# Text gate rows moved into the text output's run of 32-column matmuls, with P of batch 0 transposed ahead of text V

## The chip, the core and the metric

The kernel runs on one core of a Trainium2 chip. The metric is the device time of one execution in microseconds (us). A core has a matmul engine (TensorE, PE in the profile, with its weight loads shown as PEld), a vector engine (DVE), a scalar engine (ACT), GpSimd (POOL) and SyncE (SP); here SP does nothing but issue DMAs. Each engine works through its own queue in order and waits for the others by semaphores. Matmul results go to PSUM, and DVE and ACT bring them from there to SBUF.

## The reference

One attention block over two streams of tokens, image and text, for a batch of 2, with 256 image tokens, 32 text tokens and D = 1152, all in bf16. Each stream has its own weights and its own modulation (shift, scale and gate) from a condition vector `c`.

```
mod_i = (silu(c) @ wmod_img)            # shift, scale, gate of the image
mod_t = (silu(c) @ wmod_txt)            # shift, scale, gate of the text
hi = layernorm(x_img) * (1 + sci) + shi
ht = layernorm(x_txt) * (1 + sct) + sht
q, k, v = concat of (ht @ wqkv_txt, hi @ wqkv_img)
p = softmax(q @ k^T * D**-0.5)
a = p @ v                               # at: text rows, ai: image rows
out_i = x_img + gai * (ai @ wo_img)
out_t = x_txt + gat * (at @ wo_txt)
```

## The kernel before

The reduction dimension D is cut into KT = 9 blocks of 128. All weights come in blocks of 1152 x 1152 (2592 KB) through five SBUF slots, asked for by SP in the order of lines 80 to 122; a load waits in SP's queue until the last reader of its slot is done, and the loads behind it wait too. The last ones are the image gate (slot 0, free when DVE has read the text shift weights), text V (slot 1), the text gate (slot 2, free after text Q), the image output weights `w_o_i` (slot 3, three row groups, free after text K) and the text output weights `w_o_t` (slot 1 again, free after text V).

The order of PE's work is written out by hand: every matmul and transpose goes through `mm` (line 61) or `tr` (line 64), which pin it to program order. After image scale and V (to about 35 us) come image Q and K (`qk_img`, lines 372 to 380), with hooks between their nine column blocks at which the text preparation is put in: `txt_ln` (LayerNorm statistics on DVE), `txt_shift_part` (lines 413 to 419: the text shift vector made on DVE as 18 products of weight rows with a scalar, 1.4 us each), `txt_shift_split`, `txt_rows_scale`, `txt_rows_shift`, `txt_modulate`. Then text Q and K, and, from 77 us on, the part that matters here, in this order on PE: scores of batch 0, scores of the text rows of both batches, image gate rows, scores of batch 1, text V, transposes of P of batch 0 and of batch 1, text gate rows, attention, and the output of the four image tiles with the text output between the third and the fourth.

Work with few columns of weights is tiled over the array: the 128 columns are split into strips of 64 or 32, and matmuls with different strips run side by side. Gate rows (`mod_rows`, lines 496 to 506) multiply the silu columns `sT32` (32 columns, two of them used) with the gate weights, four strips of 288 output columns, 9 blocks: 36 matmuls. Their result stands in PSUM as a row per batch and strip, goes to SBUF (`g_sb`), from there to a DRAM scratch `gsc` by POOL's DMAs, and back as a broadcast over partitions: `gb` for the image, `gbf` for the text, where partition 64g + 32b + t holds the gate values of text token t of batch b for column group g. The text output (`out_txt`, lines 656 to 671) uses two strips of 64 columns (both batches' 32 tokens in one), two runs of 9 blocks, 18 matmuls each; DVE multiplies by `gbf`, adds `xf` (the text input in the same layout) and two DMAs write it out.

P is normalised by DVE per tile (`softmax_tile`: `nmx`, then ACT's `e` with its row sum, then `rs` and two products into `pb`). `p_transposes(b)` makes nine transposes of the two image tiles and the text tile into one PSUM tile, copied to `pT` by DVE for batch 0 and by ACT for batch 1. `v_txt` evicts its four parts alternately by DVE and ACT into `v_t`, and DVE copies `v_t` to a second set of partitions. In `attn_pair` (three output tiles of each batch at a time) the key matmuls of batch 0 come first, then six matmuls with `v_t`, batches 0 and 1 in turn, then the key matmuls of batch 1.

The scheduler orders what is not pinned (evictions, DMAs) by program order and dependences. PSUM has six buffers for matmul results (`ps_mm`) and two for transposes and strips (`ps_tr`).

Of the kernel before, what the change touches and what calls it, by code (L numbers as in the profile page):

```python
# [14 lines left out]
def kernel(  # L15
# [14 lines left out]
    nc = tc.nc  # L30
    bf = mybir.dt.bfloat16
    f32 = mybir.dt.float32
    PSUM = bass.MemoryType.PSUM

    B, NI, D = x_img.shape
    NT = x_txt.shape[1]
    P = 128
    KT = D // P
# [3 lines left out]
    NTT = B * NT  # L42
    CH = 384
    NCH = D // CH
    VC = 288
# [7 lines left out]
    work = ctx.enter_context(tc.tile_pool(name="work", bufs=2))  # L53
    small = ctx.enter_context(tc.tile_pool(name="small", bufs=4))
    ps_mm = ctx.enter_context(tc.tile_pool(name="ps_mm", bufs=6, space=PSUM))
    ps_tr = ctx.enter_context(tc.tile_pool(name="ps_tr", bufs=2, space=PSUM))
# [3 lines left out]
    def mm(*a, **k):  # L60
        return pin(nc.tensor.matmul(*a, **k))  # L61

    def tr(*a, **k):
        return pin(nc.tensor.transpose(*a, **k))  # L64
# [11 lines left out]
    def wtile(slot):  # L76
        return wpool.tile([P, KT, D], bf, tag="w%d" % slot, name="t")

    def wview(src, c0):
        return src.rearrange("(kt p) n -> p kt n", p=P)[:, :, c0:c0 + D]  # L80
# [3 lines left out]
    def load_w(slot, src, c0, splits=(D,)):  # L84
        t = wtile(slot)
        sv = wview(src, c0)
        o = 0
        for n in splits:
            nc.sync.dma_start(t[:, :, o:o + n], sv[:, :, o:o + n])
            o += n  # L90
        return t

    def load_rows(slot, src, c0):
        t = wtile(slot)
        sv = wview(src, c0)
        for r0 in range(0, KT, 3):
            nc.sync.dma_start(t[:, r0:r0 + 3, :], sv[:, r0:r0 + 3, :])
        return t
# [13 lines left out]
    w_q_i = load_w(3, wqkv_img, 0)  # L112
    w_sh_t = load_rows(0, wmod_txt, 0)
    w_k_i = load_w(4, wqkv_img, D)
# [2 lines left out]
    w_k_t = load_w(3, wqkv_txt, D)  # L117
    w_ga_i = load_w(0, wmod_img, 2 * D)
    w_v_t = load_w(1, wqkv_txt, 2 * D)
    w_ga_t = load_w(2, wmod_txt, 2 * D)  # L120
    w_o_i = load_rows(3, wo_img, 0)
    w_o_t = load_rows(1, wo_txt, 0)

    nc.scalar.preload_act_table_set("natural_log_exp_and_others")
# [4 lines left out]
    NGG = 4  # L129
# [12 lines left out]
    sT32 = const.tile([P, KT, 32], bf)  # L142
# [39 lines left out]
    def evac(out_ap, in_ap):  # L182
        if evac_idx[0] % 2 == 0:
            nc.vector.tensor_copy(out_ap, in_ap)  # L184
        else:
            nc.scalar.copy(out_ap, in_ap)  # L186
        evac_idx[0] += 1
# [36 lines left out]
    def group(w, kt, g):  # L224
        return w[:, kt, :].rearrange("p (c g l) -> p g c l", g=NGG, l=LW)[:, g]
# [140 lines left out]
    def qk_evac(out_ap, in_ap, blk):  # L366
        if blk == 0:
            nc.scalar.mul(out_ap, in_ap, SCALE)  # L368
        else:
            nc.scalar.copy(out_ap, in_ap)  # L370

    def qk_img(wq, blk, hooks):
        for j in range(KT):
            for hook in hooks.get(j, ()):
                hook()
            ps = ps_mm.tile([P, B * NI], f32, tag="mm")
            for kt in range(KT):
                mm(ps[:], lhsT=wq[:, kt, j * P:(j + 1) * P], rhs=hT_i[:, kt, :],
                   start=(kt == 0), stop=(kt == KT - 1))
            qk_evac(qkT[:, blk * KT + j, :, 0:NI], ps[:].rearrange("p (b n) -> p b n", b=B), blk)  # L380

    gsc = tc.dram_tile([2, B, D], bf, name="mod_scratch")
    sel = const.tile([P, NGG, NTT], bf)
    nc.gpsimd.tensor_scalar(sel[:].rearrange("p g (b t) -> p g b t", b=B),
                            ident[:].rearrange("p (g r) -> p g r", g=NGG)[:, :, 0:B].unsqueeze(3)
# [55 lines left out]
    def txt_shift_part(r0, r1):  # L441
        return lambda: vec_part(nc.vector, w_sh_t, acc_sh, r0, r1, range(B))
# [38 lines left out]
    def v_txt():  # L481
        for r in range(2):
            ps = ps_mm.tile([P, KT, LW], f32, tag="mm")
            for kt in range(KT):
                for g in range(2):
                    mm(ps[64 * g:64 * g + NTT], lhsT=hT_t[:, kt, :], rhs=group(w_v_t, kt, 2 * r + g),
                       start=(kt == 0), stop=False, tile_position=(0, 64 * g))
            for g in range(2):
                mm(ps[64 * g:64 * g + NTT], lhsT=sel[:, 2 * r + g, :], rhs=svr[:],
                   start=False, stop=True, tile_position=(0, 64 * g))  # L490
            for g in range(2):
                evac(v_t[0:NTT, :].rearrange("p (c g l) -> p g c l", g=NGG, l=LW)[:, 2 * r + g],
                     ps[64 * g:64 * g + NTT])
        nc.vector.tensor_copy(v_t[64:64 + NTT, :], v_t[0:NTT, :])

    def mod_rows(w_blk, si):
        gps = ps_mm.tile([P, VC], f32, tag="mm")
        for kt in range(KT):
            for g in range(NGG):
                mm(gps[32 * g:32 * g + 32, :], lhsT=sT32[:, kt, :], rhs=w_blk[:, kt, g * VC:(g + 1) * VC],  # L500
                   start=(kt == 0), stop=(kt == KT - 1), tile_position=(0, 32 * g))
        g_sb = work.tile([P, VC], bf, tag="garow")
        evac(g_sb[:], gps[:])
        for b in range(B):
            nc.gpsimd.dma_start(gsc[si, b, :].rearrange("(g j) -> g j", g=NGG), g_sb[b:P:32, :])  # L505

    gb = act.tile([P, B, D], bf, tag="Bt")
    gbf = act.tile([P, 2, VC], bf)
    xf = act.tile([P, 2, VC], bf)

    def img_gate():
        mod_rows(w_ga_i, 0)
        for b in range(B):
            nc.gpsimd.dma_start(gb[:, b, :], gsc[0, b, :].partition_broadcast(P))

    def txt_gate():
        mod_rows(w_ga_t, 1)
        for g in range(2):
            pin(nc.gpsimd.dma_start(xf[64 * g:64 * g + NTT, :, :],
                                    xt_flat.rearrange("t (r g j) -> g t r j", r=2, g=2)[g]))  # L520
            for b in range(B):
                r0 = 64 * g + 32 * b
                nc.gpsimd.dma_start(gbf[r0:r0 + NT, :, :],
                                    gsc[1, b, :].rearrange("(r g j) -> g r j", r=2, g=2)[g].partition_broadcast(NT))

    v_last()
    shift_v_rows()
    qk_img(w_q_i, 0, {1: (txt_ln,), 2: (txt_shift_part(0, 3),), 5: (txt_shift_part(3, 6),),
                      6: (txt_transposes,), 8: (txt_shift_part(6, KT),)})
    qk_img(w_k_i, 1, {1: (txt_shift_split,),  # L530
                      6: (txt_rows_scale, txt_rows_shift, txt_cols_shift, txt_modulate),
                      8: (lambda: qk_txt(0, w_q_t),)})
    qk_txt(1, w_k_t)
# [1 line left out]
    aT = act.tile([P, KT, B * NTOK], bf, tag="Q")  # L535
# [19 lines left out]
    def scores_img(b):  # L555
        for qi in range(TPB):
            q0 = qi * P
            sps = ps_mm.tile([P, NTOK], f32, tag="mm")
            for ft in range(KT):
                mm(sps[:], lhsT=qkT[:, ft, b, q0:q0 + P], rhs=qkT[:, KT + ft, b, :],  # L560
                   start=(ft == 0), stop=(ft == KT - 1))
            softmax_tile(sps, P, (b, qi), [(0, P, b)])
# [15 lines left out]
    def p_transposes(b):  # L578
        pT_ps = ps_tr.tile([P, 8 * P], bf, tag="tr")

        def one(kj, pb, qp, perm):
            o = kj * NTOK + qp
            tr(pT_ps[:, o:o + P], pb[:, kj * P:(kj + 1) * P], perm[:])

        for kj in range(3):
            if b:
                one(kj, pbs["t"], qpos[b][2], ident2)
            for qi in range(TPB):
                one(kj, pbs[(b, qi)], qpos[b][qi], ident)
            if not b:  # L590
                one(kj, pbs["t"], qpos[b][2], ident)
        pT_v = pT_ps[:, 0:3 * NTOK].rearrange("p (k n) -> p k n", k=3)
        pT = work.tile([P, 3, NTOK], bf, tag="pT")
        if b == 0:
            nc.vector.tensor_copy(pT[:], pT_v)
        else:
            nc.scalar.copy(pT[:], pT_v)
        pTs[b] = pT
# [29 lines left out]
    scores_img(0)  # L628
    scores_txt()
    img_gate()  # L630
    scores_img(1)
    v_txt()
    p_transposes(0)
    p_transposes(1)
    txt_gate()
    for d0 in range(0, KT, 3):
        attn_pair(*[[(b, dt) for dt in range(d0, d0 + 3)] for b in range(B)])

# [17 lines left out]

    def out_txt():
        of = work.tile([P, 2, VC], bf, tag="of", bufs=1)
        for r in range(2):
            ps = ps_mm.tile([P, VC], f32, tag="mm")  # L660
            for dt in range(KT):
                for g in range(2):
                    c0 = (2 * r + g) * VC
                    mm(ps[64 * g:64 * g + NTT, :], lhsT=aT[:, dt, NI:NI + NTT], rhs=w_o_t[:, dt, c0:c0 + VC],
                       start=(dt == 0), stop=(dt == KT - 1), tile_position=(0, 64 * g))
            tmp = work.tile([P, CH], bf, tag="tmp")
            nc.vector.tensor_mul(tmp[:, 0:VC], ps[:], gbf[:, r, :])
            nc.vector.tensor_add(of[:, r, :], tmp[:, 0:VC], xf[:, r, :])
        for g in range(2):
            eng = nc.sync if g == 0 else nc.scalar  # L670
            eng.dma_start(ot_flat.rearrange("t (r g j) -> g t r j", r=2, g=2)[g], of[64 * g:64 * g + NTT, :, :])
# [37 lines left out]
```

## Time and profile before

| what | value |
|---|---|
| median of 9 executions | 119.88 us (118.7 to 120.3) |
| the profiled execution | 120.22 us |
| its span, first to last instruction on the core | 118.1 us |
| PE busy | 110.8 us (94%) |
| DVE, ACT, POOL busy | 75.8, 41.8, 11.2 us |
| read from HBM | 39.38 MB, about 410 GB/s from 10 to 95 us |

The times in the profile's views run from the span's start; the execution's own time is 2.1 us more than the span. PE's granted clock is full throughout. Rows of the timeline give start, length, engine, line, operation, tiles and count; a bracket gives the idle time ahead of the row on that engine and what ended it. A matmul's length is longer than the distance to the next one, since matmuls are pipelined: costs are read from start to start.

### The profile page before, as it was taken

To read this page: it belongs to the slowest core of one execution; us is meant where nothing else is said; L and a number is where in the kernel's file an instruction comes from. 1 tells how busy PE (TensorE), PEld (TensorE's weight loads), DVE (VectorE), ACT (ScalarE), POOL (GpSimd) and SP (SyncE) were. 2 spreads that over 40 slices of the span, in tenths; PEclk is the share of its full clock that TensorE was granted. 3 is DMA by queue.
4 is the path that set the end of the run, shared out by engine and by line. 5 is a ranking of instruction groups with operands and counts; after the bars stand their busy time and mean duration, and the time that the engine had idled before them with its cause. 6 is when DMAs were issued, how large, how long until landed. Compare 5 with 4: busy or idle time off the path is not lost.

```text
span 118.1 us, 2512 instructions
## 1 busy us (share of the span) xinstructions
PE 110.8 (94%) x1046; PEld 63.9 (54%) x1054; DVE 75.8 (64%) x161; ACT 41.8 (35%) x87; POOL 11.2 (9%) x34
## 2 busy tenths in 40 slices
PE   4987799999999999999999999899999999999990
PEld 1334544445574445444444557776886566556660
DVE  2668394063866799999999740018696666666571
ACT  4899520031762423423319232245454620000000
POOL 7410000000000000000000000000409008000000
PEclk9999999999999999999999999999999999999999
DMA  3999999999999999999999999999999998320223
GB/s 112 375 391 401 404 405 411 412 412 412 412 399 373 412 412 410 405 411 413 411 413 349 381 410 410 406 414 404 414 397 412 411 394 341 138 94 11 100 50 100
DMA packets 18613, 40.86 MB, mean 346 GB/s; under 512 B 1019, under 2 KB 1547, under 8 KB 18603
## 3 DMA queue, kind: packets, MB, share of 16 engines
q1 hardware_dynamic: 17728, 39.56, 86.4%
q0 software_dynamic: 480, 0.89, 2.1%
q10 hardware_dynamic: 395, 0.26, 0.7%
q8 instruction: 8, 0.13, 0.4%
q14 instruction: 2, 0.02, 0.0%
HBM read 39.38 MB, written 1.34 MB: 345 GB/s over the span
## 4 chain that ended last, share of the span: by engine, by line
PE 85%; DMA 9%; DVE 1%; issue 1%; SPq 1%; DVEq 0%
PE ps L61 52%; PE vps L61 15%; DMA t<-in_wmod_img_dram 9%; PE gps L61 6%; PE aps L61 5%; PE sps L61 4%; PE pT_ps L64 1%; PE sc_ps L61 1%; SPq L104 1%; PE tp L64 1%; DVE tmp L650 1%; DVE o L651 0%; SPq L108 0%; PE tpt L64 0%; DVE hS_i L268 0%
## 5 line engine op out<-in xcount | busy, mean ns | idle before, releaser
L61 PE MATMUL ps<-xT_i,t 128*128 128x512 bf16 x157 | 35.4, 379 | 0.3
L61 PEld LDWEIGHTS <-t 128*128 128x128 bf16 x324 | 20.6, 98 | 19.6 <-issue 0.9
L419 DVE SCALAR_TENSOR_TENSOR acc_sh<-t,sTf,acc_sh 128x1152 f32<-128x1152 bf16 x16 | 21.4, 1413 | 0.0
L61 PE MATMUL ps<-t,aT 128*128 128x384 bf16 (+3 forms) x153 | 20.2, 308 | 0.0
L61 PE MATMUL vps<-t,hS_i 128*128 128x512 bf16 (+1 forms) x106 | 17.8, 325 | 0.2
L61 PEld LDWEIGHTS <-aT 128*128 128x128 bf16 (+1 forms) x153 | 13.0, 101 | 7.1 <-issue 0.5
L61 PEld LDWEIGHTS <-hS_i 128*128 128x128 bf16 x108 | 8.9, 97 | 8.8 <-DVE hS_i L268 0.4
L650 DVE TENSOR_TENSOR tmp<-ps,gb 128x384 bf16<-128x384 f32 (+2 forms) x13 | 6.8, 526 | 6.4 <-PE ps L61 6.3
L368 ACT ACTIVATE qkT<-ps 128x512 bf16<-128x512 f32 (+2 forms) x11 | 6.2, 561 | 11.8 <-PE ps L61 11.8
L370 ACT CAST qkT<-ps 128x512 bf16<-128x512 f32 (+2 forms) x11 | 5.9, 552 | 11.4 <-PE ps L61 11.4
L505 POOL DMA_DIRECT2D mod_scratch<-g_sb x4 | 2.6, 642 | 76.4 <-ACT g_sb L186 76.3
L61 PE MATMUL wps<-warm 128*128 128x512 bf16 x24 | 7.0, 446 | 1.6 <-DVE unit L132 1.5
L184 DVE CAST v_i<-vps 128x512 bf16<-128x512 f32 x5 | 3.5, 692 | 7.5 <-PE vps L61 7.5
L542 DVE TENSOR_REDUCE nmx<-sps 128x1 f32<-128x288 f32 x4 | 1.7, 449 | 9.4 <-PE sps L61 9.4
L61 PEld LDWEIGHTS <-sT 128*32 128x32 bf16 x180 | 4.7, 96 | 3.2 <-issue 2.4
L186 ACT CAST v_i<-vps 128x512 bf16<-128x512 f32 x4 | 2.3, 579 | 9.9 <-PE vps L61 9.9
L61 PE MATMUL gps<-t,sT 128*32 128x288 bf16 x144 | 5.5, 287 | 0.1
L61 PE MATMUL ps<-hT_t,t 128*128 128x64 bf16 x162 | 5.2, 193 | 0.4 <-issue 0.4
L61 PE MATMUL sps<-qkT 128*128 128x288 bf16 (+1 forms) x54 | 5.5, 287 | 0.0
L610 DVE TENSOR_SCALAR aT<-aps,svc 128x288 bf16<-128x288 f32 x9 | 4.3, 517 | 1.6 <-PE aps L61 1.6
L61 PEld LDWEIGHTS <-warm 128*128 128x128 bf16 x25 | 2.5, 110 | 5.0 <-issue 1.9
L61 PE MATMUL aps<-pT,v_i 128*128 128x288 bf16 x36 | 5.1, 287 | 0.0
(112 smaller groups left out, 107.5 us busy)
## 6 DMA issues: line engine op xcount, KB each, us to landing
t<-in_wqkv_txt_dram SPq DMA_DIRECT2D x3, 2592.0 KB, 17.8
t<-in_wmod_img_dram SPq DMA_DIRECT2D x2, 2592.0 KB, 11.8
t<-in_wqkv_img_dram SPq DMA_DIRECT2D x2, 2592.0 KB, 20.1
t<-in_wmod_txt_dram SPq DMA_DIRECT2D x2, 2592.0 KB, 16.1
t<-in_wmod_txt_dram SPq DMA_DIRECT2D x3, 864.0 KB, 15.0
t<-in_wo_img_dram SPq DMA_DIRECT2D x3, 864.0 KB, 12.8
t<-in_wo_txt_dram SPq DMA_DIRECT2D x3, 864.0 KB, 11.9
t<-in_wqkv_img_dram SPq DMA_DIRECT2D x3, 576.0 KB, 8.7
```

Source lines behind the costliest of these rows:

```text
L61: return pin(nc.tensor.matmul(*a, **k))
L64: return pin(nc.tensor.transpose(*a, **k))
L104: nc.sync.dma_start(x_i[:, b * TPB:(b + 1) * TPB, :], x_img[b].rearrange("(p t) d -> p t d", t=TPB))
L184: nc.vector.tensor_copy(out_ap, in_ap)
L186: nc.scalar.copy(out_ap, in_ap)
L368: nc.scalar.mul(out_ap, in_ap, SCALE)
L370: nc.scalar.copy(out_ap, in_ap)
L419: pin(eng.scalar_tensor_tensor(acc[:, b, :], w[:, kt, :], sTf[:, kt, b:b + 1], acc[:, b, :], op0=ALU.mult, op1=ALU.add))
L505: nc.gpsimd.dma_start(gsc[si, b, :].rearrange("(g j) -> g j", g=NGG), g_sb[b:P:32, :])
L542: nc.vector.reduce_max(nmx[0:qn, :], sps[0:qn, :], axis=AX.X, negate=True)
L610: nc.vector.tensor_scalar(dst, tiles[(b, dt)][:], bias, None, op0=ALU.add)
L650: nc.vector.tensor_mul(tmp[:, 0:n], ps[:, 0:n], gb[:, b, c0:c0 + n])
```

## The change

- The text gate rows are no longer made after the P transposes. `txt_gate` is gone; what is left of it, `txt_x`, loads `xf` by POOL ahead of the scores of batch 1. The text part of the scratch and its DMAs are gone.
- In `out_txt` the gate rows come first (36 matmuls in four strips of 32 columns), ACT copies them to `g_sb`, and the output's rows are made in four strips of 32 columns (36 matmuls in each of the two runs, for 18 strips of 64). Between the two runs, selector matmuls with `sel` (entries -1 at the row of strip and batch) spread the gate rows over the partitions, four for each run, and ACT multiplies them by -1 into `gbf`.
- P of batch 0 is transposed right after the scores of batch 1, ahead of text V.
- The load of `w_o_i` goes ahead of that of the text gate weights in SP's queue.
- At the hooks of image Q and K, the first three weight rows of the text shift come ahead of the text LayerNorm, and the text transposes go from image Q to image K.

```diff
     w_v_t = load_w(1, wqkv_txt, 2 * D)
+    w_o_i = load_rows(3, wo_img, 0)
     w_ga_t = load_w(2, wmod_txt, 2 * D)
-    w_o_i = load_rows(3, wo_img, 0)
     w_o_t = load_rows(1, wo_txt, 0)
...
-    gsc = tc.dram_tile([2, B, D], bf, name="mod_scratch")
+    gsc = tc.dram_tile([1, B, D], bf, name="mod_scratch")
...
-    def txt_gate():
-        mod_rows(w_ga_t, 1)
+    def txt_x():
         for g in range(2):
             pin(nc.gpsimd.dma_start(xf[64 * g:64 * g + NTT, :, :],
                                     xt_flat.rearrange("t (r g j) -> g t r j", r=2, g=2)[g]))
-            for b in range(B):
-                r0 = 64 * g + 32 * b
-                nc.gpsimd.dma_start(gbf[r0:r0 + NT, :, :],
-                                    gsc[1, b, :].rearrange("(r g j) -> g r j", r=2, g=2)[g].partition_broadcast(NT))
...
-    qk_img(w_q_i, 0, {1: (txt_ln,), 2: (txt_shift_part(0, 3),), 5: (txt_shift_part(3, 6),),
-                      6: (txt_transposes,), 8: (txt_shift_part(6, KT),)})
-    qk_img(w_k_i, 1, {1: (txt_shift_split,),
+    qk_img(w_q_i, 0, {1: (txt_shift_part(0, 3),), 3: (txt_ln,), 4: (txt_shift_part(3, 6),),
+                      7: (txt_shift_part(6, KT),)})
+    qk_img(w_k_i, 1, {1: (txt_transposes, txt_shift_split,),
                       6: (txt_rows_scale, txt_rows_shift, txt_cols_shift, txt_modulate),
                       8: (lambda: qk_txt(0, w_q_t),)})
...
     img_gate()
+    txt_x()
     scores_img(1)
+    p_transposes(0)
     v_txt()
-    p_transposes(0)
     p_transposes(1)
-    txt_gate()
...
     def out_txt():
         of = work.tile([P, 2, VC], bf, tag="of", bufs=1)
-        for r in range(2):
+        gps = ps_tr.tile([P, VC], f32, tag="tr")
+        for kt in range(KT):
+            for g in range(NGG):
+                mm(gps[32 * g:32 * g + 32, :], lhsT=sT32[:, kt, :], rhs=w_ga_t[:, kt, g * VC:(g + 1) * VC],
+                   start=(kt == 0), stop=(kt == KT - 1), tile_position=(0, 32 * g))
+        g_sb = work.tile([P, VC], bf, tag="garow")
+        nc.scalar.copy(g_sb[:], gps[:])
+        quads = [(g, b, 64 * g + NT * b) for g in range(2) for b in range(B)]
+
+        def rows_of(r):
             ps = ps_mm.tile([P, VC], f32, tag="mm")
             for dt in range(KT):
-                for g in range(2):
+                for g, b, r0 in quads:
                     c0 = (2 * r + g) * VC
-                    mm(ps[64 * g:64 * g + NTT, :], lhsT=aT[:, dt, NI:NI + NTT], rhs=w_o_t[:, dt, c0:c0 + VC],
-                       start=(dt == 0), stop=(dt == KT - 1), tile_position=(0, 64 * g))
+                    mm(ps[r0:r0 + NT, :], lhsT=aT[:, dt, NI + NT * b:NI + NT * (b + 1)], rhs=w_o_t[:, dt, c0:c0 + VC],
+                       start=(dt == 0), stop=(dt == KT - 1), tile_position=(0, r0))
+            return ps
+
+        def gate_of(r):
+            gp = ps_tr.tile([P, VC], f32, tag="tr")
+            for g, b, r0 in quads:
+                mm(gp[r0:r0 + NT, :], lhsT=sel[:, 2 * r + g, NT * b:NT * (b + 1)], rhs=g_sb[:],
+                   start=True, stop=True, tile_position=(0, r0))
+            nc.scalar.mul(gbf[:, r, :], gp[:], -1.0)
+
+        def finish(r, ps):
             tmp = work.tile([P, CH], bf, tag="tmp")
             nc.vector.tensor_mul(tmp[:, 0:VC], ps[:], gbf[:, r, :])
             nc.vector.tensor_add(of[:, r, :], tmp[:, 0:VC], xf[:, r, :])
+
+        ps = rows_of(0)
+        gate_of(0)
+        gate_of(1)
+        finish(0, ps)
+        finish(1, rows_of(1))
```

## The prediction

> **What bounds the kernel now.** I read the page's head and chain first, then the chain in order of time, then the timeline from 60 us on. In the first fence PE is busy for 94% of the span and the chain that ended last is 85% PE.
>
> ```profile
> span 118.1 us, 2512 instructions
> PE 110.8 (94%) x1046; PEld 63.9 (54%) x1054; DVE 75.8 (64%) x161; ACT 41.8 (35%) x87; POOL 11.2 (9%) x34
> ...
> PE 85%; DMA 9%; DVE 1%; issue 1%; SPq 1%; DVEq 0%
> ```
>
> The chain in order of time (start, length, what) shows where the change lies: text V, the P transposes, the text gate rows and attention follow one another on PE with no other engine between, and from 94.90 us PE alone runs to the tail.
>
> ```profile
> 84.12 2.57 PE ps L61 x40
> 86.69 1.11 PE pT_ps L64 x18
> 87.80 1.22 PE gps L61 x36
> 89.01 5.88 PE aps L61 x54
> 94.90 19.52 PE ps L61 x144
> ```
>
> So a matmul taken out or put in counts in full, unless it covers a wait. The timeline (start, length, engine, what; single starts named below are read from the same trace) gives the prices and, on DVE and ACT, what the gate rows cover today.
>
> ```profile
> 64.46 1.29 PE L61 MATMUL gps<-t,sT 128*32 128x288 bf16 x36
> ...
> 65.57 0.66 PE L61 MATMUL gps<-hl,pick 128*32 128x288 bf16 x16
> ...
> 83.61 0.49 DVE L551 TENSOR_SCALAR pbt<-e,rs 32x64 bf16<-32x64 f32 x2
> 84.04 1.00 PEld L61 LDWEIGHTS <-hT_t 128*64 128x64 bf16 x18 [0.24 <-issue]
> ...
> 85.31 0.16 DVE L547 RECIPROCAL rs<-rs 128x1 f32<-128x1 f32 x1 [0.35 <-ACT e L545]
> 85.51 0.35 DVE L549 TENSOR_SCALAR pb<-e,rs 128x256 bf16<-128x256 f32 x1
> ...
> 87.05 0.76 ACT L186 CAST v_t<-ps 64x288 bf16<-64x288 f32 x2 [1.28 <-DVE v_t L184]
> ...
> 87.33 0.61 DVE L595 COPY pT<-pT_ps 128x864 bf16<-128x864 bf16 x1
> ...
> 87.83 0.88 ACT L597 COPY pT<-pT_ps 128x864 bf16<-128x864 bf16 x1
> ...
> 89.79 0.42 PE L61 MATMUL aps<-pT,v_t 32*128 32x288 bf16 x6
> ...
> 107.99 2.10 PEld L61 LDWEIGHTS <-aT 128*64 128x64 bf16 x36 [0.32 <-issue]
> ```
>
> Two things are to be seen. First, four 32-column strips run side by side: 36 matmuls of 288 columns take 65.57 - 64.46 = 1.11 us, nine sets of four at 0.123 us, and a set of two 64-column strips costs as much (18 loads from 84.04 to the next form at 85.05). Second, ACT copies P of batch 1 (87.83 to 88.71) while PE makes the gate rows (87.73 to 88.95), and PE reads that copy at 89.79. The gate rows hide it.
>
> **The change, part by part** (against the profiled execution: 118.1 us of span, 120.22 us; that is 0.34 us above the median of 119.88 us).
>
> 1. Gate rows leave the middle. From the last P transpose (87.58) to the first attention matmul (88.95) is 1.37 us; without the gate a transpose pitch of about 0.06 us is left. Gain 1.31 us, if nothing was hidden under it: nine sets are 1.10 us, the change into 32-column strips and out of them about 0.1 us each.
>
> 2. The text output. Today 18 sets of two and one change of form: 107.99 to 110.31, 2.32 us. Then nine gate sets, nine and nine output sets (the same rows, now 32 columns at a time, four strips for two), and two selector sets: 29 sets, 11 more than today: 11 x 0.123 = +1.35 us. All 29 have one form, so no change of form is added. The selector matmuls need the gate rows in SBUF: last gate set + 0.29 us + an ACT copy of 0.40 us, and the 1.10 us of the first output run covers that; without the cover it would cost about 0.7 us. ACT's two products of some 0.4 us and DVE's four end before out_img(3) does; ACT has nothing else there.
>
> 3. Parts 1 and 2 alone are +0.04 us. What decides is P of batch 0 ahead of text V. Changes of form stay two, so PE pays nothing for the move itself. But DVE copies this P, and in the built order the copy (0.61 us) stands behind the reciprocal of batch 1's first tile and ahead of batch 1's four P products and the two text V evictions. Copy: 85.47 to 86.08; the products at 85.51 go to 86.08, +0.57 us; DVE's first V eviction from 86.57 to 87.14; ACT's, which waits for it, from 87.05 to 87.62; and ACT's copy of P of batch 1, behind it on ACT, from 87.83 to 88.40, ending at 89.28.
>    PE meanwhile: the last score matmul starts at 83.83; the third transpose waits for pbt (ready at 84.10) about 0.15 us; text V starts at 84.70 for 84.05, the second transposes at 87.27 (their P is ready then, 86.98 + 0.25 = 87.23), batch 0's key matmuls at 87.79 and, as today 0.84 us later, the text matmuls at 88.63. Of the six, the second needs P of batch 1: 89.28 and a hand-over of 0.05 us. So PE stands for 0.70 us behind the first, all later matmuls queued behind it. Key matmuls follow 0.35 us on, at 89.68 instead of 90.14. The middle thus gains 0.46 us, not 1.31.
>    Bounds of the wait: 0 if the copy fell into DVE's 0.35 us of idleness ahead of the reciprocal (then at most 0.26 us of delay remains, and part of the wait with it); 1.0 us if text V also loses a little. The order forbids the first, so I take 0.70, with 0.4 and 1.0 as ends.
>
> 4. Loads. w_o_i is asked for at 77.45 as before, when its slot comes free; the gate weights, asked for at 72.62 today, go behind it and are read only near 107.6 us. In the text V load (needed at 84.05) nothing changes, w_o_i comes earlier by one load (2592 KB, some 6.4 us at 410 GB/s), w_o_t is asked for 0.65 us later and takes 10 to 13 us: 100 us, against 108.7. The output's start does not wait for w_o_i today (PE goes from aps to ps without a gap at 94.7), so the earlier landing gains 0. POOL loses six issues (two scratch writes, four gate broadcasts) behind nothing that waits for them; gb lands at 88.54 + 6.8 = 95.3 us and is first read at about 95.9. If it came 1 us late, DVE (0.92 us of each 1.46 us chunk) would catch up within six PSUM buffers. 0.
>
> 5. The DVE order of text LayerNorm and shift: three weight rows first, then statistics. The sum of DVE's work is the same; today it starts at 37.05 (x_txt lands), then at 37.1 (first shift rows: issue 17.5 + 19.6). acc_sh ends at 63.1 as before, and with it w_ga_i's issue. The halves are used 0.2 us before PE would wait. 0; from 0 to +0.5 us. ACT's rstd now stands ahead of the fifth q eviction, up to 0.8 us late, within PSUM's six buffers: 0. The five text transposes move by 7 us on PE, same form, same cost.
>
> Sum: -1.31 + 0.85 (wait 0.70, pbt 0.15) + 1.35 = +0.89 us: span 119.0, 121.1 us as the profiled execution counts, 120.8 us against the median.
>
> [...]
>
> **The rivals.**
> - R1, slower by over 1%: the early DVE chain. Today the shift rows have 3 us of slack (landed 37.1, first read 40.27); then they have none. If they land later than 37.3, the halves, PE's 16 pick matmuls at 65.57 and all behind them move one for one, and DMA, which already runs dry near 64 us (349 GB/s in that slice), waits longer for w_ga_i. For it: both landing times lie under a loaded DMA (405 GB/s in that slice) and can shift. Against: in this execution x_txt (37.05) and the shift rows (37.1) land together, so DVE starts as late today. At 0.5 us later it gives +1.2 us, 121.1 and up.
> - R2, no wait for P: 0 to +0.3 us, 119.9 to 120.2. It needs ACT's copy done by 88.6, 0.7 us sooner than worked out; only a later text V start on PE or faster evictions give part of that.
> - R3, faster: PE stands twice for want of instructions (rows at 75.60, 0.46 idle, and at 81.73, 0.59 idle with 0.24 usual). If those stalls come from a loaded DMA, and the gate weights not queued at 72.62 take them away, 0.7 us comes off: with the wait +0.2, without it -0.7 us, 119.2. Against: 63 to 79 us is full of w_ga_i and w_v_t anyway.
> - R4, the spread of strips or the selectors stall PE (g_sb late): +0.3 to +0.7 more, 121.1 to 121.5. Against: 0.4 us of cover is left.
>
> **How the numbers follow.** Likeliest case 0.58 (+0.5 to +1.25 us: 120.4 to 121.1); R1 0.12; R4 0.06; R2 0.14; R3 0.10. A measurement of this kernel tells about 1%, 1.2 us, from no change. Slower by over 1%: R1, R4 and a quarter of the likeliest, 0.33. Faster by over 1% only if R3 comes whole and more: 0.06. Within 1%: 0.61. The single runs of before lie from 118.7 to 120.3, so a median can shift by 0.7 us either way; the range takes R3's and R2's values and R4's: 119.2 to 121.8.
>
> **What would show it.** Right: gate rows gone from between pT_ps and aps; an idle of 0.5 to 0.9 us on PE at the first aps<-pT,v_t, released by ACT's pT copy, which starts near 88.4; keys at 89.7; 116 strip matmuls in a row of about 3.6 us before out_img(3); span near 119.0. Wrong: no such idle (R2), pick matmuls later than 65.8 (R1), the two issue gaps gone (R3), a set longer than 0.13 us in the text output (the rule, R4).

## The result, and the profile after

The changed kernel takes 119.9 us (median of 18 executions, 119.14 to 120.57). The kernel before, run beside it, takes 119.2 us (55 executions, 118.27 to 120.52). The ratio is 1.0057 with a 95% interval from 1.0035 to 1.0079: 0.7 us slower, between 0.4 and 0.9 us. The nine executions shown before the prediction had a median of 119.88 us, 0.7 us above that of the larger sample. The profile shown with them (120.22 us) is one of the slow executions of this kernel, whose fastest took 118.27 us.

The page of the changed kernel has the same span as the one shown before, 118.1 us, and PE's share of the chain that ended last has fallen from 85% to 77%; DVE and ACT have taken it over.

```profile
span 118.1 us, 2594 instructions
PE 111.2 (94%) x1090; PEld 64.4 (55%) x1098; DVE 75.0 (64%) x160; ACT 43.3 (37%) x90; POOL 7.9 (7%) x28
...
PE 77%; DMA 8%; DVE 6%; ACT 3%; issue 1%; SPq 1%; ACTq 0%; DVEq 0%
```

The same span is a coincidence of two profiles: the one of before holds 0.88 us of waits of PE that end in "issue", that is, are released by nothing that the profile shows, beyond the usual 0.24 us of a change of form; a second profile of the same kernel does not have them (experiment 4). I call them issue waits; the recorded texts call them waits for instructions, which was my reading of them and is not shown. To compare stages I take distances from start to start inside each profile: from the last score matmul to batch 1's first key matmul of attention (the stretch, below), and the text output.

The chain in order of time shows where PE lost the lead. From 77.88 to 88.46 us it runs over the softmax tiles on DVE and ACT, the text V evictions and the copy of P; here are its last pieces.

```profile
84.64 0.16 DVE rs L542
84.80 0.51 DVE pT L590
85.31 0.26 DVE pb L544
85.57 0.17 DVE pb L546
85.73 0.08 DVE rs L542
85.84 0.35 DVE pb L544
86.19 0.16 DVE pb L546
86.35 0.37 DVE v_t L184
86.75 0.76 ACT v_t L186 x2
87.53 0.89 ACT pT L592
88.46 5.09 PE aps L61 x47
```

The copy of P of batch 0 (DVE, pT) stands between the reciprocal and batch 1's products, and everything behind it follows without a gap until PE may go on. In the timeline the first text matmul starts at 87.57 and the second, which reads P of batch 1, at 88.46:

```profile
86.74 0.90 PE L61 MATMUL aps<-pT,v_i 128*128 128x288 bf16 x6
...
87.53 0.88 ACT L592 COPY pT<-pT_ps 128x864 bf16<-128x864 bf16 x1
...
87.57 0.29 PE L61 MATMUL aps<-pT,v_t 32*128 32x288 bf16 x1
...
88.46 0.40 PE L61 MATMUL aps<-pT,v_t 32*128 32x288 bf16 x5 [0.60 <-ACT pT L592]
```

The six text matmuls take 1.02 us from first to last start, for 0.14 before: a wait of 0.88 us. The whole stretch takes 6.00 us for 6.31.

The text output is one run of strips, as the weight loads of the timeline show (start, length, count):

```profile
106.65 0.98 PEld L61 LDWEIGHTS <-sT 128*32 128x32 bf16 x36 [0.32 <-issue]
...
107.64 1.09 PEld L61 LDWEIGHTS <-aT 128*32 128x32 bf16 x36
...
107.99 0.40 ACT L660 CAST g_sb<-gps 128x288 bf16<-128x288 f32 x1 [13.89 <-PE gps L61]
108.74 0.23 PEld L61 LDWEIGHTS <-sel 128*32 128x32 bf16 x8
...
108.99 1.09 PEld L61 LDWEIGHTS <-aT 128*32 128x32 bf16 x36
...
110.31 2.23 PEld L61 LDWEIGHTS <-aT 128*128 128x128 bf16 x15 [0.24 <-issue]
```

From 106.65 to 110.31 are 3.66 us, for 2.32 before, and ACT's copy for the selectors (107.99 to 108.39) is done before they start: +1.34 us and no wait. So PE's path is longer by 1.34 - 0.31 = 1.03 us. From the first V matmul to the last matmul, the changed kernel's later two profiles (experiment 4) have 100.08 us each (the first has 100.16, with 0.07 us of issue wait), and two of the old arrangement without issue waits (the kernel before again, and the one with the new hooks alone) 99.06 us each: 1.0 us.

### The profile page after: what moved, and what is told of

Same layout as the page of the kernel before. It is cut to its first block, busy times and chain, and to the rows that moved or that the text cites. A ratio compares the mean times of both kernels' runs of the same rounds, so it can differ in the third digit from the quotient of the medians.

```text
span 118.1 us, 2594 instructions
## 1 busy us (share of the span) xinstructions
PE 111.2 (94%) x1090; PEld 64.4 (55%) x1098; DVE 75.0 (64%) x160; ACT 43.3 (37%) x90; POOL 7.9 (7%) x28
## 4 chain that ended last, share of the span: by engine, by line
PE 77%; DMA 8%; DVE 6%; ACT 3%; issue 1%; SPq 1%; ACTq 0%; DVEq 0%
PE ps L61 50%; PE vps L61 15%; DMA t<-in_wmod_img_dram 8%; PE gps L61 5%; PE aps L61 4%; ACT e L540 2%; DVE nmx L537 1%; PE sps L61 1%; PE sc_ps L61 1%; DVE pb L544 1%; ACT pT L592 1%; SPq L104 1%; PE tp L64 1%; ACT v_t L186 1%; DVE rs L542 1%
## 5 line engine op out<-in xcount | busy, mean ns | idle before, releaser
L61 PE MATMUL wps<-warm 128*128 128x512 bf16 x24 | 7.5, 465 | 1.7 <-DVE unit L132 1.5
L505 POOL DMA_DIRECT2D mod_scratch<-g_sb x2 | 1.4, 692 | 74.9 <-ACT g_sb L186 74.9
```

## The experiments

**1. Which part of the wait is the order of P and text V, and which the copies?** Three kernels. The first puts text V back ahead of both transposes:

```diff
-    p_transposes(0)
     v_txt()
+    p_transposes(0)
     p_transposes(1)
```

> The changed kernel with text V ahead of both P transposes, as before. My theory (the wait for ACT's copy of P of batch 1 behind text V's evictions costs 0.9 us): that wait goes; instead the first key matmul waits some 0.35 us for DVE's copy of P of batch 0. From the last score matmul to batch 1's first key matmuls 5.35 us, for 5.96 us in the changed kernel's profile and 6.31 us in that of before: 0.6 us faster than the changed kernel, ratio to before 0.999 to 1.002. Rival (the loss is in the text output alone, and the wait at the copy is slack elsewhere): no change, 1.005 to 1.007.

Ratio 1.0026 (0.9996 to 1.0056). The stretch takes 5.67 us, 0.33 less than the 6.00 of the changed kernel; I expected 5.35. The text matmuls no longer wait (0.14 us from first to last), and ACT copies P of batch 1 without holding up PE. The wait has moved to the first key matmul, which now needs DVE's copy of P of batch 0:

```profile
86.79 0.59 DVE L590 COPY pT<-pT_ps 128x864 bf16<-128x864 bf16 x1
...
87.44 0.91 PE L61 MATMUL aps<-pT,v_i 128*128 128x288 bf16 x6 [0.51 <-DVE pT L590]
88.28 0.42 PE L61 MATMUL aps<-pT,v_t 32*128 32x288 bf16 x6
```

So the rival that the wait is slack is wrong by the stretch (the ratio's interval alone would still allow it), and my size for the next wait (0.35) was too small. With the text gate rows gone, either order of P and text V leaves PE standing.

The second kernel keeps the order and swaps the engines of the two copies:

```diff
-        if b == 0:
+        if b == 1:
             nc.vector.tensor_copy(pT[:], pT_v)
```

> The changed kernel with ACT copying P of batch 0 (it has nothing to do then) and DVE P of batch 1. My theory: DVE's batch 1 products and text V evictions run 0.6 us earlier, P of batch 1 is copied by about 87.6 us in the changed kernel's time, and the wait moves to the second half of v_t, which DVE copies after it: about 0.5 us of wait for 0.9. So 0.3 to 0.4 us faster than the changed kernel, ratio 1.002 to 1.004. Rival (the wait is ACT's own, set by its evictions): no change or slower, 1.005 to 1.008.

Ratio 1.0009 (0.9981 to 1.0038). The stretch takes 5.53 us, 0.47 less, and the six text matmuls 0.53 us for 1.02. ACT copies P of batch 0 in time in which it did nothing, DVE's chain runs ahead, and what is left is a wait for the second half of `v_t`, which DVE copies after P of batch 1:

```profile
87.26 0.61 DVE L590 COPY pT<-pT_ps 128x864 bf16<-128x864 bf16 x1 [0.15 <-PE pT_ps L64]
...
87.90 0.45 DVE L494 COPY v_t<-v_t 64x1152 bf16<-64x1152 bf16 x1
...
88.41 0.30 PE L61 MATMUL aps<-pT,v_t 32*128 32x288 bf16 x4 [0.21 <-DVE v_t L494]
```

The third takes that wait away as well, by letting the first attention group read the first half alone:

```diff
-    def attn_pair(ids0, ids1):
+    def attn_pair(ids0, ids1, halves_of_v=2):
...
-            r0 = 64 * (n // 2 % 2) + NT * b
+            r0 = 64 * (n // 2 % halves_of_v) + NT * b
...
-        attn_pair(*[[(b, dt) for dt in range(d0, d0 + 3)] for b in range(B)])
+        attn_pair(*[[(b, dt) for dt in range(d0, d0 + 3)] for b in range(B)], halves_of_v=1 if d0 == 0 else 2)
```

> The changed kernel with the copies of P swapped (ACT batch 0, DVE batch 1), and the first attention group's six text matmuls on the first half of v_t alone, so that they need not wait for DVE's second half. My theory: the 0.4 us that was left of the wait goes, a third set of strips costs 0.12 us; from the last score matmul to batch 1's first key matmuls 5.2 to 5.3 us (5.53 with the copies swapped alone, 6.00 in the changed kernel); ratio 0.999 to 1.002. Rival (another wait comes next, on P of batch 1 itself): 5.5 us and no gain over the swapped copies.

Ratio 0.9989 (0.9963 to 1.0016). The stretch takes 5.22 us, 0.78 less than in the changed kernel. The text matmuls take 0.27 us and nothing waits there:

```profile
86.64 0.61 DVE L590 COPY pT<-pT_ps 128x864 bf16<-128x864 bf16 x1 [0.15 <-PE pT_ps L64]
...
87.27 0.55 PE L61 MATMUL aps<-pT,v_t 32*128 32x288 bf16 x6
...
87.28 0.45 DVE L494 COPY v_t<-v_t 64x1152 bf16<-64x1152 bf16 x1
...
87.75 1.64 PE L61 MATMUL aps<-pT,v_i 128*128 128x288 bf16 x12
```

The three ratios fall in the order of the three stretches, though their intervals overlap; only the last lies clear of the changed kernel's (1.0035 to 1.0079). This last kernel does what the changed one does without its wait, and it is level with the kernel before, not better: 1.34 us in the text output against 6.31 - 5.22 = 1.09 us in the middle.

**2. Is it the gate rows that hid the wait before?** The kernel before, with P of batch 0 ahead of text V and nothing else (the same two lines of the diff).

> The kernel before with P of batch 0 transposed ahead of text V and nothing else. My theory: ACT's copy of P of batch 1 is late by 0.6 us here too, but the text gate rows still stand between the transposes and attention and cover it: no idle at the first text matmuls; from the last score matmul to batch 1's first key matmuls 6.4 us (6.31 before), ratio 1.000 to 1.002. Rival (the move costs its wait wherever the gate rows are): 7.0 us or more, ratio 1.005 to 1.008.

Ratio 1.0002 (0.9976 to 1.0029). The stretch takes 6.31 us as before, for my 6.4: the 0.1 us that I had put down for the wait for pbt (P of the text rows) is not there, because this profile has an issue wait of 0.35 us ahead of the last scores (experiment 4), in which pbt became ready. DVE's copy stands in the same place and ACT's copy behind text V's evictions as in the changed kernel, but the gate rows lie over it:

```profile
86.76 1.29 PE L61 MATMUL gps<-t,sT 128*32 128x288 bf16 x36
...
87.31 0.88 ACT L597 COPY pT<-pT_ps 128x864 bf16<-128x864 bf16 x1
...
87.98 0.91 PE L61 MATMUL aps<-pT,v_i 128*128 128x288 bf16 x6
...
88.83 0.42 PE L61 MATMUL aps<-pT,v_t 32*128 32x288 bf16 x6
```

The copy ends at 88.19 and its reader starts at 88.83: 0.64 us to spare, and still 0.3 us if the issue wait were not there and the scores' end 0.35 us earlier. So the earlier P costs nothing by itself; it costs 0.88 us where the gate rows are gone.

**3. The parts put down at nothing.** The hooks alone, in the kernel before:

```diff
-    qk_img(w_q_i, 0, {1: (txt_ln,), 2: (txt_shift_part(0, 3),), 5: (txt_shift_part(3, 6),),
-                      6: (txt_transposes,), 8: (txt_shift_part(6, KT),)})
-    qk_img(w_k_i, 1, {1: (txt_shift_split,),
+    qk_img(w_q_i, 0, {1: (txt_shift_part(0, 3),), 3: (txt_ln,), 4: (txt_shift_part(3, 6),),
+                      7: (txt_shift_part(6, KT),)})
+    qk_img(w_k_i, 1, {1: (txt_transposes, txt_shift_split,),
```

> The kernel before with the new hooks alone (three weight rows of the text shift ahead of the text LayerNorm, text transposes in image K). My theory: the same DVE work starting at the same landing time, ratio 0.998 to 1.002. Rival (the shift rows have no slack left and often land late): slower, 1.003 and up. Rival (the earlier end of the shift lets the image gate's load start sooner and DMA run dry less): 0.995 to 0.998.

Ratio 0.9983 (0.9954 to 1.0012): no difference that can be told. The pick matmuls of the text shift start 50.83 us after the first V matmul in this profile, in that of before, and in that of the changed kernel.

The text output's rows in four strips for two, in the kernel before:

```diff
-                for g in range(2):
+                for g, b, r0 in [(g, b, 64 * g + NT * b) for g in range(2) for b in range(B)]:
                     c0 = (2 * r + g) * VC
-                    mm(ps[64 * g:64 * g + NTT, :], lhsT=aT[:, dt, NI:NI + NTT], rhs=w_o_t[:, dt, c0:c0 + VC],
-                       start=(dt == 0), stop=(dt == KT - 1), tile_position=(0, 64 * g))
+                    mm(ps[r0:r0 + NT, :], lhsT=aT[:, dt, NI + NT * b:NI + NT * (b + 1)], rhs=w_o_t[:, dt, c0:c0 + VC],
+                       start=(dt == 0), stop=(dt == KT - 1), tile_position=(0, r0))
```

> The kernel before with the text output's rows in four strips of 32 columns for two of 64, the gate rows left where they are. My reading of the rows: 18 sets as before, text output 2.42 us from the third image tile's last matmul to the fourth's first less a pitch, ratio 0.999 to 1.001. Rival (the weight loads of column strips do not overlap, 36 more of them at 0.096 us): the text output 3 us or more longer, ratio 1.025 and up.

Ratio 1.0004 (0.9973 to 1.0035). Twice as many loads lie in the same time: 72 in 2.08 us, for 36 in 2.10 before, 2.32 us from start to start in both.

```profile
106.56 2.08 PEld L61 LDWEIGHTS <-aT 128*32 128x32 bf16 x72 [0.32 <-issue]
108.88 2.06 PEld L61 LDWEIGHTS <-aT 128*128 128x128 bf16 x14 [0.24 <-issue]
```

**4. Load order, and the issue waits in the profile of before.** In that profile PE's weight loads stand twice longer than usual with no releaser but "issue": 0.46 us ahead of 75.60, inside one form, and 0.59 ahead of 81.73, where the other changes from strips back to full width from 64 us on show 0.23 or 0.24. On PE's path they cost 0.53 and 0.35 us:

```profile
75.60 1.70 PEld L61 LDWEIGHTS <-t 128*128 128x128 bf16 x56 [0.46 <-issue]
77.23 2.09 PEld L61 LDWEIGHTS <-qkT 128*128 128x128 bf16 x18
79.56 0.48 PEld L61 LDWEIGHTS <-qkT 128*32 128x32 bf16 x18 [0.24 <-issue]
79.94 1.20 PEld L61 LDWEIGHTS <-sT 128*32 128x32 bf16 x36
81.73 0.36 PEld L61 LDWEIGHTS <-qkT 128*128 128x128 bf16 x4 [0.59 <-issue]
```

In the profile of the changed kernel both are gone. Was that the load order?

```diff
+    w_ga_t = load_w(2, wmod_txt, 2 * D)
     w_o_i = load_rows(3, wo_img, 0)
-    w_ga_t = load_w(2, wmod_txt, 2 * D)
```

> The changed kernel with the loads back in the old order (text gate weights ahead of the image output weights). Theory F: the two instruction waits of PE that the profile of before shows near 75 and 81 us (0.53 and 0.24 us longer pitch than usual) come with the gate weights' load in the DMA queue at 72.6 us; they come back, and the ratio to before rises from 1.0057 to about 1.010 to 1.012. Rival: those waits are chance and go with no part of the change; ratio 1.004 to 1.008, as the changed kernel. In both the wait of 0.9 us at the first text matmuls of attention stays.

Ratio 1.0034 (1.0003 to 1.0065), and neither wait is in its profile. So Theory F, that the waits come whenever the gate weights are queued there, fell. Then the kernel before once more:

> The kernel before, unchanged, for a second profile. Chance theory: the two instruction waits of PE near 75 and 81 us in the first profile of before (0.53 and 0.24 us) are not there, from the last scores' first matmul to the last 6.22 us for 6.57, and the span is about 117.3 us. Rival: they belong to this kernel's load order, and are there again.

118.73 us, span 116.6 us, neither wait: the scores' matmuls take 6.22 us. The loads at the place of the second wait now read:

```profile
78.84 1.20 PEld L61 LDWEIGHTS <-sT 128*32 128x32 bf16 x36
80.28 1.71 PEld L61 LDWEIGHTS <-qkT 128*128 128x128 bf16 x15 [0.24 <-issue]
```

So the waits come and go between executions of one kernel. With `b_hooks` (none), experiment 2 and the strips' kernel (the second wait, 0.35 us, in both), three of five profiles of the old arrangement hold the second wait, and one the first as well. In each of the three, one of the packets of the instruction queue q8 (8 of 16,384 bytes each in the profile of before, blocks below) starts at 71.8 to 73.2 us, in the other two at 68.6 and 69.5. That these blocks hold PE's instructions, as the expectations have it, is my reading too: the profile gives the queue and its kind alone. Four more profiles, two of each load order, asked whether the order changes the size of that wait:

> The changed kernel, unchanged, a second profile, for the instruction wait of PE at the end of the image gate rows (0.35 us in three profiles of the old load order, each time with an instruction block of PE fetched near 72 us instead of 69). Theory: with the new load order the next block's fetch starts some 0.5 us sooner after it, and the wait is under 0.1 us or none even where the block before came late. Rival: the load order has no part in it, and a late block brings 0.35 us here too. In both: first V matmul to the last matmul 100.1 us without instruction waits (99.06 in the kernel before), and 0.88 us of wait at the second text matmul.

> As for the profile just before, a third one of the same kernel.

> The changed kernel with the loads in the old order, a second profile. Theory: where a block of PE's instructions comes late (near 72 us), 0.35 us of wait at the end of the image gate rows; none where it comes near 69 us. Rival (load order has no part): waits of the same size as in the changed kernel's profiles.

> As for the profile just before, a third one of the same kernel.

In the two of the changed kernel (120.44 and 120.31 us) the block came near 69 us and there was no wait, so the question about the size got no answer from them. Two profiles shown above do answer it. With the new load order, the block came late in the first profile of the changed kernel (72.66 us) and in that of the kernel with one half of `v_t` (72.29 us). Their loads at the place of the second wait, in this order:

```profile
80.70 2.07 PEld L61 LDWEIGHTS <-qkT 128*128 128x128 bf16 x18 [0.24 <-issue]
80.44 2.08 PEld L61 LDWEIGHTS <-qkT 128*128 128x128 bf16 x18 [0.32 <-issue]
```

The wait is nothing in one and 0.08 us in the other, for 0.35 in each of the four profiles with a late block and the old load order (the fourth follows). The next block starts 5.1 and 5.5 us after the late one, for 5.8 to 6.1 with the old loads. So this wait goes with the load order where the block is late, as the theory had it, and the first profile of the changed kernel and the one that follows differ in nothing but that order. The new order does not keep the block from coming late. These are six profiles, and how the load order acts on the block was not shown.

Of the two with the old loads, one (120.53 us) had the late block (73.15 us) and the wait, and shows what I had not thought of. Its weight loads in text K and at the end of the image gate rows:

```profile
75.56 1.70 PEld L61 LDWEIGHTS <-t 128*128 128x128 bf16 x56 [0.19 <-issue]
...
81.69 0.85 PEld L61 LDWEIGHTS <-qkT 128*128 128x128 bf16 x8 [0.59 <-issue]
```

The text matmuls, of the same profile's timeline:

```profile
88.42 0.29 PE L61 MATMUL aps<-pT,v_t 32*128 32x288 bf16 x1
89.11 0.40 PE L61 MATMUL aps<-pT,v_t 32*128 32x288 bf16 x5 [0.39 <-ACT pT L592]
```

The scores take 6.57 us for 6.22, but the stretch behind them 5.65 for 6.00: the sum is 12.22 us with the second wait and without. It is swallowed by the wait for P, since the chain over DVE and ACT runs on meanwhile. The first wait, 0.25 us here, lies ahead of the scores and is not: from the first V matmul to the last matmul this profile has 100.35 us, for 100.08. In the kernel before the 0.35 us of the second wait count in full (6.57 + 6.31 for 6.22 + 6.31). The other old-order profile (120.54 us) had no issue wait, but a late `w_o_i`:

```profile
93.73 1.14 PE L61 MATMUL ps<-t,aT 128*128 128x384 bf16 x6
95.05 1.14 PE L61 MATMUL ps<-t,aT 128*128 128x384 bf16 x6 [0.18 <-DMA t<-in_wo_img_dram]
```

The image output took 0.34 us more there (21.63 us from its first matmul to the last, for 21.29). The changed kernel starts its output 0.24 to 0.32 us sooner after the first V matmul than the kernel before without issue waits. With the old loads this cost nothing in two of three profiles and 0.34 us in one; the ratios (1.0034 and 1.0057) do not tell the two load orders apart.

## Why the prediction was right in kind and off in size

Point by point, against the sum:

- Gate rows out of the middle, -1.31 us if nothing was hidden: something was, as the prediction said. The place (the second text matmul), the releaser (ACT's copy) and the cause (DVE's copy of P of batch 0 ahead of batch 1's products) are as forecast, and experiments 1 and 2 show them.
- The wait: 0.70 us forecast, with ends at 0.4 and 1.0; it is 0.88 us (0.60 in the row's bracket, since a matmul's length is longer than the distance to the next). PE came to the first text matmul 4.77 us after the last score matmul, not 4.80, and ACT's copy ended 0.17 us later than worked out (5.62 us after it, not 5.45).
- The pbt wait of 0.15 us: about 0.1 us in the changed kernel's transposes (0.10 and 0.13 us from one to the next where 0.056 is usual), and without effect, since a longer wait follows.
- The middle gained 0.31 us, not 0.46. This term of the sum was mis-sized by 0.15 us.
- Text output +1.35 us: +1.34. The selectors' wait is covered.
- Loads 0: in the changed kernel's three profiles with the old order, the late `w_o_i` cost nothing in two and 0.34 us in one.
- Hooks 0: right. R1 did not happen; DVE starts on the shift rows at 36.73 us, 0.98 us idle for their landing.
- R4, and loads of column strips that do not overlap (the rival of the strips' kernel, and "the rule" among the signs): neither. In that kernel 72 loads of column strips take 2.08 us, for 36 in 2.10 before, and the 29 sets of the changed kernel's text output start from 106.65 to 110.09 us, 0.123 us a set.

PE's path thus became 1.0 us longer where 0.89 was forecast, by the waits and the matmuls that were forecast. Yet the measured difference is 0.7 us (0.4 to 0.9), and the time 119.9 us where 120.8 stands. Two steps failed.

The first is the base. The sum was put on a median of nine, which lay 0.7 us above that of 55; the prediction had itself allowed a median to shift by as much. Beside the first group of experiments the kernel before had a median of 119.83 us (35 executions), beside the second, on another chip, 119.22 (29). Against 119.2 us, 120.8 us is a rise of 1.3%; the measured one is 0.6%.

The second is that the sum took the waits in the one profile of before for the kernel's own. The 0.88 us of issue waits stood in its span of 118.1 us and were carried over to the changed kernel's 119.0; only R3 had them go, with 0.7 us and a chance of 0.10. But the second profile of before has neither wait and is 1.46 us shorter: 0.88 us of that is the waits, and 0.57 lies ahead of the first V matmul (at 14.74 us in the first profile, 14.17 in the second). The changed kernel's three profiles have 0.07 us of such waits, none and none, and spans of 118.1, 118.4 and 118.3 us. So R3's sign, the two issue gaps gone, came together with the signs of the likeliest case. R3's reason, the load order, holds in part: in experiment 4 the second wait is smaller with the new order where the block is late, but the waits are missing in half of the eight profiles with the old order too. That a loaded DMA makes them, R3's condition, was not shown.

What the waits do to the measured difference can only be estimated. From the first V matmul to the last matmul the five profiles of the old arrangement have 99.38 us on average and the changed kernel's three 100.11, which is 0.73 us and near the measured 0.7. Eight profiles are few, and that this share of waits holds over the timed executions was not shown; why it is 0.7 and not 1.0 us stays open so far.

R2 (no wait) did not happen in the changed kernel, though the measured 119.9 us falls into its band of 119.9 to 120.2: that is luck, and comes of the lower base. Being level with before is what the kernel with swapped copies and half of `v_t` shows.

## What to carry to other kernels

Work that is taken from the bounding engine in the middle of a kernel may be the cover of a chain on other engines; before it is moved, follow the next reader's data back and see when it would be ready without it. The same matmuls cost the same elsewhere (nine sets here, 1.1 us, and two sets more for the spread), so a move pays only by what it hides. Small waits do not add up along the path: a wait on PE ahead of a wait for DVE and ACT can be swallowed by it, as 0.35 us were here, and two profiles of one kernel can differ by more than the change does (1.46 us, for 0.7). A single profile of a kernel is therefore no base for a forecast of 1%.

## What the runs showed of the hardware

- Two or four column strips of 288 columns cost the same per set here, 0.123 us (nine sets of two in text V from 84.05 us, nine of four in the gate rows from 64.46, both in the profile of before), with the weights of every strip loaded each time (72 loads in 2.08 us and 36 in 2.10, experiment 3). The change from full width to strips and back costs about 0.1 us each: 0.22 us to the next start (83.83 to 84.05 and 65.95 to 66.17 in the profile of before), for 0.123 within a form.
- PE stood where the profile shows no releaser: in the first profile of before twice, for 0.53 and 0.35 us of its path, and in the second not at all. After the waits of 0.35 us the next form's loads start some 2.5 us after a block's packet (79.27 and 81.73; 79.13 and 81.69; both in kernels with the text gate weights queued in the old order). In the profiles with the early block this wait is absent, and in the two with a late block and the new load order it is nothing and 0.08 us; in the four with a late block and the old order it is 0.35. That the late block causes the wait is read from these profiles, where no wait came without it; no run here set it.
